# Two orderings moved in a two-layer attention and gated-MLP kernel: a first V pass of five contraction steps, and block 1's score sums held behind a layer norm

## The chip, the cores and the metric

The kernel runs on one core of a Trainium2 chip. The metric is the device time of one execution in microseconds (us); lower is better. Before the change it was 1618.4 us, the median of 3 executions (1618.09 to 1618.7). The profile's span (first to last instruction) is 1.7 to 2.0 us shorter than the device time in nearly all executions, and 2.6 to 2.7 us in three.

## The reference

Two layer pairs; each is attention over a dilated local window of 8 keys, then a gated MLP. S = 2048, D = 1024, F = 3584, 32 heads of 32.

```python
x = A_x
x = x + _A_ref(_layernorm(x), A_wqkv, A_wo)                    # q, k, v; 8 keys, 2 apart; softmax; @ wo
x = x + _B_ref(_layernorm(x), B_W_gate, B_W_up, B_W_down)      # (relu(x @ Wg) * (x @ Wu)) @ Wd
x = x + _A_ref(_layernorm(x), A_wqkv, A_wo)
x = x + _B_ref(_layernorm(x), B_W_gate, B_W_up, B_W_down)
return x
```

## The kernel before

The 2048 rows are worked on in four blocks of 512 rows (four tiles of 128 each). TensorE (PE) does all projections. VectorE (DVE) does the attention of one block while PE does the MLP of another. Q, K and V are the attention's input projections, Wo its output projection, LN2 the layer norm between Wo and the MLP; gate, up and down are the MLP's projections. PSUM is the memory that PE's products land in, and the other engines copy them out. The order on each engine is fixed by hand: `dv`, `mm` and `sp_dma` chain every operation behind the last one of its engine, and the program is emitted from a list of events with nominal times.

```python
def sp_dma(dst, src, transpose=False):
    start = nc.sync.dma_start_transpose if transpose else nc.sync.dma_start
    ...
        with tc.issue_after(tail_sp[0]):          # all these DMAs stand in ONE queue, in order
            tail_sp[0] = start(dst, src).ins
```

The start. Four tiles are normalised and turned (transposed) on PE, tile by tile; the V projection begins on tile 0 while the others are still being normalised.

```python
# ln_first: engine "v" is DVE, "a" is ACT, "g" is GpSimd
act_square(2)
act_mean(2)                       # ACT, two passes over tile 2
bn(1, 0)
apply(0, 0); apply(0, 1)          # normalise tile 0
turn(0)                           # 8 PE transposes
copy(0, "a", 0, 0, KC // 4)       # ACT copies the turned tile out of PSUM, in quarters
copy(0, "a", 0, KC // 4, KC // 2)
bn(1, 1); aggr(1)
copy(0, "v", 1)
act_power(2)
apply(1, 0); apply(1, 1)
...
def head():                       # V products of tile 0: contraction steps 0 to 3
    for kc in range(KC // 2):
        if kc == KC // 2 - 1:
            ln["second"](0)       # turn the first half of tile 1, copy it (DVE)
        for c in range(KC):
            prod(kc, c, 0, 1)
    ln["second"](1)               # turn the second half of tile 1
```

The V weights come in four pieces of two contraction steps each (512 KB): pieces 0 and 1, then x tile 3, then pieces 2 and 3.

Block 1's scores. `prod_sum_steps(1)` gives 16 steps; each is one multiplication of 128x2048 on DVE and mostly one addition, 2.2 to 2.3 us apiece. Steps 0 to 7 make the first half of the sums, 8 to 15 the second half. The second half is stored to DRAM and read back in another layout; head sums, softmax and the product with V follow.

```python
spread(sums1[:4], t_pv0 + 34.5, 4.5)
spread(sums1[4:6], t_wo0 + 0.5, 2.5)        # steps 4, 5: in front of the Wo additions
spread(sums1[6:10], t_fill + 1.4, 4.6)      # step 6: in front of tile 3's normalisation
spread(sums1[10:], t_gu0 + 2.6, 5.4)
...
# in gate/up of block 0; `at` is its start
ev.append((at + 37.5, store_s(1, 1)))       # second half of the sums -> DRAM
ev.append((at + 40.5, load_s(1)))           # read back, four DMAs
spread(gets2, at + 36.0, 2.5)               # block 2's q and k tiles
```

Weights come as slabs of 1 MB into a ring of five buffers. Gate and up each have seven slabs; a slab serves four of the 28 column groups of 128.

## Time and profile before

| before | value | read from |
|---|---|---|
| device time | 1618.4 us | 3 executions |
| PE busy | 1611.3 of 1616.4 us | busy table |
| 512-column matmul, start to start | 216 ns | trace |
| 256-column / 128-column matmul | 109 / 56 ns | trace |
| first Q matmul to last matmul | 1589.14 us | trace |

From the page of the kernel before: busy us (share of the span) and instructions of PE, and the chain of work that ended last, by engine.

```profile
PE 1611.3 (100%) x7633; PEld 786.6 (49%) x7633; DVE 1137.1 (70%) x960; ACT 475.8 (29%) x968; POOL 180.4 (11%) x168
...
PE 99%; DMA 0%; ACT 0%; DVE 0%; issue 0%; ACTq 0%; DVEq 0%
```

PE is the bound. The Trainium skill ("TensorE: Matmul & The Clock Gate", section "Wait — 56ns, not 53.3ns?") puts a warm matmul's start-to-start distance at N / 2.4 GHz plus about 2.5 ns and gives 215.7 and 55.6 ns as measured for 512 and 128 columns; for 256 columns an estimate from its formula is 109.2 ns. The trace's 216, 109 and 56 ns agree. Below, "against the pace" means: later than these distances allow. A change can gain only where PE falls behind that pace or has less to multiply.

The timeline of PE at the start (start in us, duration in us, engine, line, operation, out<-in, shape, count; in brackets the idle time before it and what ended it):

```profile
6.97 0.72 PE L385 MATMUL tp<-ident,xn_first 128*128 128x128 bf16 x8
8.09 1.50 PE L132 MATMUL acc_v<-xnT_first,w_v 128*128 128x128 bf16 x24 [0.40 <-ACT xnT_first L328]
9.51 0.40 PE L385 MATMUL tp_pair<-ident,xn_first 128*128 128x128 bf16 x4
9.74 0.61 PE L132 MATMUL acc_v<-xnT_first,w_v 128*128 128x128 bf16 x8
10.42 0.38 PE L385 MATMUL tp_pair<-ident,xn_first 128*128 128x128 bf16 x4
...
23.88 1.46 PE L132 MATMUL acc_q<-xnT_first,w_qk_q 128*128 128x512 bf16 x6
```

`tp` and `tp_pair` are the turns of tiles 0 and 1. The first V product waits for ACT's copy. Small waits follow before each half of tile 1's turn (9.51 and 10.42). Against the pace these are 0.55, 0.08 and 0.23 us.

The timeline of DVE around LN2 of block 0, with the same columns: the first Wo additions, the normalisations of tiles 1 and 3, and the last addition of the second sum.

```profile
168.77 2.48 DVE L106 TENSOR_TENSOR x<-acc_wo,x 128x512 bf16<-128x512 f32 x4
...
173.61 0.55 DVE L106 TENSOR_SCALAR xn_b<-x,mv,rstd 128x1024 bf16<-128x1024 bf16 x1 [0.73 <-POOL rstd L301]
...
185.35 0.54 DVE L106 TENSOR_SCALAR xn_b<-x,mv,rstd 128x1024 bf16<-128x1024 bf16 x1
...
228.38 2.29 DVE L106 TENSOR_TENSOR s<-ac,t 128x2048 bf16<-128x2048 f32 x1
```

### The profile page before, as it was taken

The numbers are of one execution on the slowest core, as the hardware profiler recorded it, in microseconds if no ns is written. First come the engines' busy times: TensorE is split into PE (matmuls) and PEld (weight loads), VectorE is DVE, ScalarE is ACT, GpSimd is POOL, SyncE is SP. The second block draws the span as 40 slices with busy tenths as digits, with TensorE's granted clock in tenths as the row PEclk, the third lists the DMA queues.
The fourth block names the chain that finished last, engine by engine and source line by source line (L and its number), as shares of the span: only waits on it lengthen the run. The fifth ranks groups of instructions, "written<-read, shape, count | busy, mean of one in ns | idle before, by whom it ended". The sixth has DMA issues, their size and how long they took to land.

```text
span 1616.4 us, 18930 instructions
## 1 busy us (share of the span) xinstructions
PE 1611.3 (100%) x7633; PEld 786.6 (49%) x7633; DVE 1137.1 (70%) x960; ACT 475.8 (29%) x968; POOL 180.4 (11%) x168
## 2 busy tenths in 40 slices
PE   9999999999999999999999999999999999999999
PEld 6646544444444445444454444544445444444444
DVE  5999989996989698929489293893939939311211
ACT  5853312132116313603136031361313311131110
POOL 2400100010003002300053000530005100000000
PEclk9999999999999999999999999999999999999999
DMA  9868868697669766794847947479574794755452
GB/s 306 180 190 238 224 159 262 183 216 204 208 192 217 200 184 212 192 246 146 227 160 201 240 153 230 152 205 252 165 226 155 203 245 157 209 161 177 157 167 68
DMA packets 407448, 317.92 MB, mean 197 GB/s; under 512 B 166464, under 2 KB 387008, under 8 KB 406848
## 3 DMA queue, kind: packets, MB, share of 16 engines
q1 hardware_dynamic: 406784, 316.13, 69.9%
q8 instruction: 59, 0.97, 0.3%
q10 hardware_dynamic: 576, 0.59, 0.1%
q14 instruction: 29, 0.24, 0.0%
HBM read 266.29 MB, written 34.66 MB: 186 GB/s over the span
## 4 chain that ended last, share of the span: by engine, by line
PE 99%; DMA 0%; ACT 0%; DVE 0%; issue 0%; ACTq 0%; DVEq 0%
PE acc_u L132 24%; PE acc_g L132 24%; PE dacc L132 18%; PE acc_v L132 7%; PE acc_wo L132 7%; PE acc_k L132 7%; PE acc_q L132 7%; PE dacc_pair L132 6%; DMA x<-in_A_x_dram 0%; ACT xn_first L328 0%; PE tp_pair L385 0%; PE L L132 0%; DVE x L837 0%; DVE xnT_first L106 0%; ACTq L175 0%
## 5 line engine op out<-in xcount | busy, mean ns | idle before, releaser
L132 PE MATMUL acc_g<-xnT_b,w_g 128*128 128x512 bf16 x1792 | 423.3, 379 | 0.0
L132 PE MATMUL acc_u<-xnT_b,w_u 128*128 128x512 bf16 x1792 | 423.3, 379 | 0.0
L790 ACT ACTIVATE r<-acc_g 128x512 bf16<-128x512 f32 x224 | 133.5, 596 | 726.7 <-PE acc_g L132 701.6
L106 DVE TENSOR_TENSOR hT<-acc_u,r 128x512 bf16<-128x512 f32 x224 | 150.5, 685 | 240.7 <-PE acc_u L132 238.2
L132 PE MATMUL dacc<-w_d,hT 128*128 128x512 bf16 (+1 forms) x1400 | 301.9, 375 | 0.0
L132 PEld LDWEIGHTS <-hT 128*128 128x128 bf16 x1820 | 178.1, 98 | 208.9
L132 PEld LDWEIGHTS <-w_u 128*128 128x128 bf16 x1792 | 175.3, 98 | 211.5
L132 PEld LDWEIGHTS <-w_g 128*128 128x128 bf16 x1792 | 175.4, 98 | 211.4
L106 DVE TENSOR_TENSOR pv<-a,vhm 128x4096 bf16<-128x4096 bf16 x64 | 143.4, 2281 | 0.0
L837 DVE TENSOR_TENSOR x<-dacc,x 128x512 bf16<-128x512 f32 (+1 forms) x38 | 24.5, 672 | 154.2 <-PE dacc L132 154.2
L608 DVE TENSOR_TENSOR t<-q,k 128x2048 f32<-128x2048 bf16 x56 | 128.0, 2292 | 6.7 <-ACT k L543 4.6
L106 DVE TENSOR_TENSOR t<-q,k 128x2048 f32<-128x2048 bf16 x56 | 127.4, 2285 | 3.7 <-ACT k L543 2.6
L106 DVE TENSOR_TENSOR pv<-pv 128x1024 bf16<-128x1024 bf16 (+1 forms) x128 | 113.6, 947 | 0.0
L549 POOL COPY kh<-k 128x14 bf16<-128x14 bf16 x40 | 56.0, 1406 | 504.3 <-ACT k L543 504.3
L132 PE MATMUL acc_wo<-w_o,oT 128*128 128x512 bf16 x512 | 111.8, 379 | 0.0
L621 DVE TENSOR_TENSOR ac<-ac,t 128x2048 f32<-128x2048 f32 x48 | 109.6, 2284 | 0.3
L106 DVE TENSOR_TENSOR ac<-ac,t 128x2048 f32<-128x2048 f32 x48 | 109.5, 2282 | 0.0
L264 POOL TENSOR_TENSOR st_b<-st_b,neg_half 128x1 f32<-128x1 f32 x29 | 43.9, 1523 | 525.8 <-ACT st_b L263 525.7
L132 PE MATMUL dacc_pair<-w_d,hT 128*128 128x512 bf16 x420 | 95.9, 379 | 0.0
L132 PEld LDWEIGHTS <-oT 128*128 128x128 bf16 x512 | 50.0, 98 | 60.4
L259 ACT ACTIVATE xn_b<-x 128x1024 bf16<-128x1024 bf16 x29 | 30.3, 1045 | 129.1 <-DVE x L106 67.0
L446 ACT CAST vT<-acc_v 128x512 bf16<-128x512 f32 x56 | 32.8, 588 | 57.6 <-PE acc_v L132 56.6
(134 smaller groups left out, 1230.0 us busy)
## 6 DMA issues: line engine op xcount, KB each, us to landing
w_g<-in_B_W_gate_dram SPq DMA_DIRECT2D x56, 1024.0 KB, 7.4
w_u<-in_B_W_up_dram SPq DMA_DIRECT2D x56, 1024.0 KB, 5.5
w_d<-in_B_W_down_dram SPq DMA_DIRECT2D x48, 1024.0 KB, 5.7
w_o<-in_A_wo_dram SPq DMA_DIRECT2D x16, 1024.0 KB, 7.0
vhm<-v_d SPq DMA_DIRECT2D x32, 284.0 KB, 6.8
v_d<-vT SPq DMA_DIRECT2D x8, 1024.0 KB, 9.8
oT<-o_d SPq DMA_DIRECT2D x32, 256.0 KB, 4.5
w_d<-in_B_W_down_dram SPq DMA_DIRECT2D x16, 512.0 KB, 3.9
```

The costliest lines, as they stand in the source:

```text
L106: tail_dve[0] = f(*args, **kwargs).ins
L132: tail_pe[0] = nc.tensor.matmul(*args, **kwargs).ins
L259: nc.scalar.activation(xn, xt[:], ACT.Square, accum_out=sq)
L264: nc.gpsimd.tensor_tensor(rstd, vpe, neg_half[:, 0:1], op=ALU.pow)
L446: tail_act[0] = nc.scalar.copy(st["vT"][:, c, :], acc[:]).ins
L549: nc.gpsimd.tensor_copy(khalo[n][:, c, :], k[:, BLK:BLK + HALO])
L608: nc.vector.tensor_tensor(t[:], i0, i1, op=ALU.mult)
L621: nc.vector.tensor_tensor(o, ac[:], t[:], op=ALU.add)
L790: tail_act[0] = nc.scalar.activation(rs[j][:], acc[:], ACT.Relu).ins
L837: run = dv if n < NB - 2 else (lambda f, *args, **kwargs: f(*args, **kwargs))
```

## The change

Its intent, at the start: let PE do a fifth contraction step of tile 0 where it waits for tile 1, so that eight later 256-column products shrink to 128 columns; take ACT's mean of tile 2 out of the way of the first copies. At LN2: let DVE do the Wo additions and normalisations of block 0 as soon as Wo's results come, and do block 1's sum steps 5 and 6 after that.

```diff
         act_square(2)
-        act_mean(2)
 ...
         copy(0, "a", 0, KC // 4, KC // 2)
+        act_mean(2)
         bn(1, 1)
         aggr(1)
         copy(0, "v", 1)
-        act_power(2)
 ...
             copy(1, "v", 1)
+            act_power(2)
             apply(2)
@@ head
-            for kc in range(KC // 2):
-                if kc == KC // 2 - 1:
+            for kc in range(KC // 2 + 1):
+                if kc == KC // 2:
                     ln["second"](0)
@@ second_half
-                        prod(kc, c, t0, t0 + 2)
+                        prod(kc, c, t0 + int((kc, t0) == (KC // 2, 0)), t0 + 2)
@@ block 1's sums
-    spread(sums1[4:6], t_wo0 + 0.5, 2.5)
-    spread(sums1[6:10], t_fill + 1.4, 4.6)
+    ev.append((t_wo0 + 0.5, sums1[4]))
+    spread(sums1[5:10], t_fill + 3.3, 3.4)
```

## The prediction

> **What bounds the kernel.** TensorE. The page's busy table gives PE 100% (1611.3 of 1616.4 us), DVE 70%; the chain that ended last is 99% PE. In the trace 512-column matmuls start every 216 ns, 256-column ones every 109, 128-column ones every 56. The Trainium skill ("TensorE: Matmul & The Clock Gate", section "Wait — 56ns, not 53.3ns?") gives N/2.4 GHz plus 2.5 ns, 215.7 and 55.6 ns; the trace agrees. From the first transpose on, places where PE ran over 40 ns behind that pace sum to about 1.1 us: 0.55 (first V product waits for ACT's first copy of tile 0, which stands behind the mean of tile 2), 0.08 among the transposes, 0.08 (tile 1's turn waits for its normalisation, 9.50 us), 0.23 (second half of the turn waits for DVE's copy of the first half, ending 10.36), 0.19 at the attention head sum. Wo, fill and gate/up of block 0 run at exactly 216 ns. The change can gain under 1 us.
>
> **First part.** ACT's mean of tile 2 (1.06 + 0.19 us, 6.63 to 7.77) moves behind the two copies. The fourth transpose starts at 7.15; with the 0.26 us that a copy takes to follow, the first copy runs about 7.41 to 7.75 and the first V product starts about 7.8 instead of 8.09. PE then has 32 products (1.79 us) instead of 24 before tile 1's turn, which starts about 9.6 (before 9.50): the wait is filled. The fifth contraction step (8 x 56 ns) needs the third piece of the V weights, landed at 10.14 in this trace, 0.3 us after PE would want it; so that step runs about 10.2 to 10.65 and the second half of the turn starts about 10.65 (before 10.42). Repaid later: eight 256-column matmuls become 128-column, 8 x 53 = 0.42 us. Net gain about 0.2 us (0.4 if the weights land early, 0 if late). Tile 2's normalisation moves from 11.2 to 12.7, needed at 14.2: harmless.
>
> **Second part.** Two DVE operations (4.5 us) go from before the Wo additions to after LN2, and another pair from before tile 3's normalisation to after it. DVE adds tile 0 at 164.4 instead of 168.8; the last transpose is issued about 178.5 instead of 185.9 (used at 190.3). PE did not wait there, so nothing is gained in this trace; margins grow (a PSUM buffer for Wo's last tile came free 0.1 us before its use). In exchange DVE waits for Wo tiles, so the held sums end about 1.1 us later (193.7, before 192.6), and the first gate product ends about 203.2; its PSUM buffer is needed at 204.1. Margin 0.9 us: no stall, but the closest risk.
>
> **Predicted time:** 1618.1 us (1618.4 - 0.2, perhaps 0.1 for margins), 80% range 1617.3 to 1619.0. Faster by over 2%: 0.005; within 2%: 0.99; slower by over 2%: 0.005.
>
> **What would show it.** Timeline: first V product at 7.8 us; a wait on the third V weight piece near 9.8 to 10.2; first Q product of block 0 about 0.2 us before 23.88. DVE: Wo additions from 164, last LN2 transpose issued before 180; block 1's first sums ending 1 us later; gate/up still at 216 ns.
>
> **What would make it wrong.** The third weight piece landing much later; DVE over 0.9 us further behind at the gate products, stalling PE 1 to 2 us; or unprofiled executions having stalls at Wo that the change removes (gain up to 1 us).

## More of the kernel before

The timeline of the DMA queue (SPq) during gate/up of block 0. For a DMA the duration is that of its issue.

```profile
218.57 0.53 SPq L121 DMA_DIRECT2D q<-q_d  x1
230.70 0.34 SPq L121 DMA_DIRECT2D s_d<-s  x1
...
233.90 4.38 SPq L121 DMA_DIRECT2D s<-s_d  x4
238.32 1.46 SPq L121 DMA_DIRECT2D q<-q_d  x1
239.88 0.39 SPq L121 DMA_DIRECT2D w_u<-in_B_W_up_dram  x1
```

The queue stands still from 219 to 230.7 us. It waits for DVE's second sum, which began at 228.38. The store, a k tile, the four read-backs and a q tile are issued next, and only then the up slab, at 239.88. This slab is the fifth of `w_u`. PE starts on it at 247.27, without a gap, in the timeline of PE:

```profile
245.54 1.89 PE L132 MATMUL acc_g<-xnT_b,w_g 128*128 128x512 bf16 x8
247.27 1.89 PE L132 MATMUL acc_u<-xnT_b,w_u 128*128 128x512 bf16 x8
```

The slab's last DMA engine reported at 246.88 us and PE loaded its first weights from it at 247.05 (landings and single matmuls are worked out from the trace's records here and below). The margin is 0.17 us in this execution.

## The result, and the profile after

The changed kernel took 1619.16 us, median of 6 executions (1618.38 to 1620.38); the kernel before took 1618.28 (1617.72 to 1618.7, 6 executions). The ratio is 1.0006, with a 95% interval of 0.9993 to 1.0019. A ratio is the mean time of one kernel's runs over that of the other's of the same rounds, so it is not quite the ratio of the medians quoted here. By the interval alone it is no difference; by the medians it is 0.9 us longer, and a repetition (below) gave 1.1 us. The profiled execution was the fastest of the six (1618.38 us), so it can show only a part of this. The median lies 0.16 us above the predicted range.

From the page after (busy row of PE, and the chain that ended last by engine):

```profile
PE 1608.1 (99%) x7592; PEld 786.4 (49%) x7641; DVE 1137.4 (70%) x960; ACT 475.8 (29%) x968; POOL 178.5 (11%) x168
...
PE 97%; DVE 1%; DMA 1%; SPq 0%; issue 0%; DVEq 0%
```

DVE and DMA have entered the chain with 1% each, and SPq is named, where the chain was 99% PE before. PE's busy time is not to be compared: this trace lacks matmul records (7592, against 7641 weight loads).

The timeline of PE at the start, after:

```profile
6.50 0.72 PE L385 MATMUL tp<-ident,xn_first 128*128 128x128 bf16 x8 [0.30 <-DVE xn_first L106]
7.36 1.95 PE L132 MATMUL acc_v<-xnT_first,w_v 128*128 128x128 bf16 x32
9.14 0.39 PE L385 MATMUL tp_pair<-ident,xn_first 128*128 128x128 bf16 x4
10.12 0.62 PE L132 MATMUL acc_v<-xnT_first,w_v 128*128 128x128 bf16 x8 [0.59 <-DMA w_v<-in_A_wqkv_dram]
10.57 0.39 PE L385 MATMUL tp_pair<-ident,xn_first 128*128 128x128 bf16 x4
...
23.61 1.67 PE L132 MATMUL acc_q<-xnT_first,w_qk_q 128*128 128x512 bf16 x7
```

The first 32 V products now run before tile 1's turn. The fifth step is the eight products at 10.12, and it waited for a piece of the V weights (0.59 us idle in the line; 0.75 us against the pace). The first Q product came at 23.61 instead of 23.88. This whole execution also started earlier: the first transpose was at 6.50 instead of 6.97. Counted from that transpose the first Q product came after 17.11 us, where it had been 16.91, so the 0.27 us on the clock are not a gain of the first part.

The timeline of DVE around LN2, after:

```profile
163.97 1.88 DVE L106 TENSOR_TENSOR x<-acc_wo,x 128x512 bf16<-128x512 f32 x3
166.05 0.69 DVE L106 TENSOR_TENSOR x<-acc_wo,x 128x512 bf16<-128x512 f32 x1 [0.20 <-PE acc_wo L132]
...
169.76 0.55 DVE L106 TENSOR_SCALAR xn_b<-x,mv,rstd 128x1024 bf16<-128x1024 bf16 x1 [1.39 <-POOL rstd L301]
...
177.81 0.55 DVE L106 TENSOR_SCALAR xn_b<-x,mv,rstd 128x1024 bf16<-128x1024 bf16 x1 [0.66 <-POOL rstd L301]
...
229.92 2.29 DVE L106 TENSOR_TENSOR s<-ac,t 128x2048 bf16<-128x2048 f32 x1
```

The Wo additions start at 163.97 instead of 168.77 and tile 3 is normalised at 177.81 instead of 185.35, as intended. But DVE now idles for a Wo tile (0.20 us) and longer for GpSimd: 1.39 us before tile 1's normalisation (0.73 before), 0.67 before tile 2's (0.66 before) and 0.66 before tile 3's (none before). These idle times grew by 1.53 us in all, and the second sum's last addition starts at 229.92 instead of 228.38. Against PE, which was 0.27 us earlier here, DVE is 1.8 us later.

The timeline of the DMA queue, after:

```profile
218.31 0.53 SPq L121 DMA_DIRECT2D q<-q_d  x1
232.24 0.34 SPq L121 DMA_DIRECT2D s_d<-s  x1
...
235.46 3.72 SPq L121 DMA_DIRECT2D s<-s_d  x4
239.23 1.26 SPq L121 DMA_DIRECT2D q<-q_d  x1
240.59 0.39 SPq L121 DMA_DIRECT2D w_u<-in_B_W_up_dram  x1
```

Everything behind the store has moved with it. The up slab is issued at 240.59, 0.98 us later against PE. That is less than DVE's 1.8 us, because in this execution the queue took 8.35 us from the store to the slab, where it took 9.18 in the kernel before (the read-backs alone 3.72 instead of 4.38). It landed at 247.50 us. The timeline of PE there, after:

```profile
245.28 1.89 PE L132 MATMUL acc_g<-xnT_b,w_g 128*128 128x512 bf16 x8
247.55 1.90 PE L132 MATMUL acc_u<-xnT_b,w_u 128*128 128x512 bf16 x8 [0.38 <-DMA w_u<-in_B_W_up_dram]
```

A gap has opened that was not there; against the pace it is 0.54 us. The waits of PE, after (us in total, times, longest):

```profile
PE acc_v L132 <- DMA w_v<-in_A_wqkv_dram: 0.6, 1, 0.6
PE acc_u L132 <- DMA w_u<-in_B_W_up_dram: 0.4, 1, 0.4
```

The balance of the profiled execution closes. From the start of the first Q matmul to the start of the last matmul it took 1589.70 us, where the kernel before took 1589.14. The difference, 0.56 us, is the gap at 247 within rounding. The first Q product was 0.27 us earlier on the clock; 0.56 - 0.27 gives 0.29 us, and the last matmul came at 1613.31 instead of 1613.02.

### The profile page after: what moved, and what is told of

The parts are those of the page before. It is cut to its first block, busy times and chain, and to the rows that moved or that the text cites. A ratio compares the mean times of both kernels' runs of the same rounds, so it can differ in the third digit from the quotient of the medians. Undisturbed runs are those within 1.5% of the kernel's fastest.

```text
span 1616.7 us, 18896 instructions
## 1 busy us (share of the span) xinstructions
PE 1608.1 (99%) x7592; PEld 786.4 (49%) x7641; DVE 1137.4 (70%) x960; ACT 475.8 (29%) x968; POOL 178.5 (11%) x168
## 4 chain that ended last, share of the span: by engine, by line
PE 97%; DVE 1%; DMA 1%; SPq 0%; issue 0%; DVEq 0%
PE acc_u L132 23%; PE acc_g L132 23%; PE dacc L132 18%; PE acc_q L132 7%; PE acc_k L132 7%; PE acc_wo L132 7%; PE acc_v L132 7%; PE dacc_pair L132 6%; DVE t L106 1%; DVE ac L106 1%; DMA w_u<-in_B_W_up_dram 0%; DMA w_v<-in_A_wqkv_dram 0%; SPq L121 0%; DMA s_d<-s 0%; DVE s L106 0%
```

## The experiments

Twelve kernels ran, each five times, with nine executions of the kernel before on the same chip; kernels with the same number in the third column share these nine. All were correct. Theory A: the held sums make DVE late, and the store that waits for DVE stands at the head of an in-order DMA queue in front of the up slab. Theory B: the first pass loses, by its wait for the third piece of the V weights, and the rest is noise.

| kernel | median us (range) | before, same chip | ratio (95%) |
|---|---|---|---|
| whole change, again | 1619.20 (1618.35 to 1619.78) | 1618.07 | 1.0005 (0.9992 to 1.0017) |
| first part alone | 1618.11 (1617.64 to 1619.26) | 1618.07 | 1.0000 (0.9988 to 1.0013) |
| second part alone | 1618.93 (1618.53 to 1620.02) | 1618.07 | 1.0004 (0.9991 to 1.0018) |
| change, two slabs in front of the store | 1622.33 (1621.44 to 1622.65) | 1618.07 | 1.0024 (1.0011 to 1.0037) |
| before, up slab later in the queue | 1618.61 (1618.46 to 1620.11) | 1617.92 | 1.0006 (0.9992 to 1.0020) |
| first part, one sum step held | 1618.52 (1618.42 to 1619.13) | 1617.92 | 1.0004 (0.9992 to 1.0017) |
| change, up slab in front of the store | 1618.14 (1617.78 to 1618.89) | 1617.92 | 1.0001 (0.9989 to 1.0014) |
| one step held, up slab and third piece early | 1617.74 (1617.47 to 1617.82) | 1617.92 | 0.9998 (0.9985 to 1.0011) |
| before, up slab in front of the store | 1618.28 (1617.67 to 1618.63) | 1618.27 | 1.0000 (0.9988 to 1.0013) |
| first part, third piece early | 1618.14 (1617.69 to 1618.74) | 1618.27 | 1.0000 (0.9986 to 1.0013) |
| change, up slab and third piece early | 1617.80 (1617.31 to 1618.13) | 1618.27 | 0.9997 (0.9984 to 1.0010) |
| first part, up slab and third piece early | 1618.26 (1617.90 to 1618.74) | 1618.27 | 1.0000 (0.9988 to 1.0013) |

Only the fourth row's interval excludes 1. The device times alone would settle little, so the next table gives what the profiled execution of each kernel shows. The columns are worked out from the traces: the landing of the piece of the V weights with contraction steps 4 and 5 (its last DMA engine), the first Q matmul, their difference, and the time from the first Q matmul to the last matmul.

| kernel | piece landed | first Q | Q - landing | last matmul - Q |
|---|---|---|---|---|
| before | 10.14 | 23.88 | 13.74 | 1589.14 |
| second part alone | 11.21 | 24.04 | 12.83 | 1589.93 |
| before, up slab later | 10.42 | 23.44 | 13.02 | 1590.08 |
| before, up slab in front | 10.82 | 24.07 | 13.25 | 1589.14 |
| whole change | 10.07 | 23.61 | 13.54 | 1589.70 |
| whole change, again | 10.04 | 23.64 | 13.60 | 1589.93 |
| first part alone | 10.35 | 23.89 | 13.54 | 1589.14 |
| first part, one step held | 10.99 | 24.54 | 13.54 | 1589.14 |
| change, up slab in front | 10.02 | 23.56 | 13.54 | 1589.14 |
| change, two slabs in front | 10.76 | 24.30 | 13.54 | 1592.19 |
| one step held, both repairs | 9.80 | 23.34 | 13.54 | 1589.14 |
| first part, third piece early | 10.32 | 23.86 | 13.54 | 1589.14 |
| change, both repairs | 10.29 | 23.83 | 13.54 | 1589.14 |
| first part, both repairs | 10.50 | 24.05 | 13.55 | 1589.14 |

Two constants stand out. Without a gap, everything after the first Q takes 1589.14 us, also with DVE 1.8 us late. With the first part of the change, the first Q comes 13.54 us after the third piece lands, in nine of ten profiled executions (13.55 counted with them), and 13.60 in the tenth. One thing is not constant: the margin of the fifth up slab. In the two other kernels that have the store and the slab at their old places and DVE on time ("first part alone" and "first part, third piece early") the slab landed 1.06 and 0.70 us before its use, where it was 0.17 in the kernel before; the queue took 8.49 and 8.54 us from the store to the slab there.

### The whole change again

No edit.

> The changed kernel again, for the same chip as the next three. Theory A (the held sums make DVE late, the store of block 1's second sum waits for DVE at the head of SP's in-order queue, and the load of the fifth up slab stands behind it and lands late): 0.5 to 1.5 us over the kernel before, a PE gap of 0.3 to 2 us in front of the first up product of that slab at about 247 us, and a wider spread than before because the landing varies. Theory B (the first pass loses: the third piece of the V weights is waited for, the rest is noise): the same total, but no gap at 247 is needed.

Measured: 1619.20 us against 1618.07, 1.1 us over, a gap of 0.77 us at 247 and the slab landed at 247.76. The spans of its five executions are 1616.6 to 1618.1 us. The size of the loss repeats. This profile, too, is of one of the faster executions (1618.64 us). The gap's size varies from one execution to the next; it was 0.54 and 0.77 us in the two that were profiled.

### First part alone

```diff
-    ev.append((t_wo0 + 0.5, sums1[4]))
-    spread(sums1[5:10], t_fill + 3.3, 3.4)
+    spread(sums1[4:6], t_wo0 + 0.5, 2.5)
+    spread(sums1[6:10], t_fill + 1.4, 4.6)
```

> First part of the change alone; the sums stand as in the kernel before. Theory A: 0.2 to 0.3 us below the kernel before (about 1618.0), PE waits 0.6 to 0.8 us for the third V piece near 9.5 us and none over 0.2 us at 247. Theory B: as slow as the whole change, 0.5 to 1 us over before.

Measured: 1618.11 against 1618.07. The wait for the third piece is there (0.63 us against the pace) and there is no gap at 247; the slab landed at 246.01. By medians and by the profile (1589.14 us after the first Q) the first part does not lose, so theory B falls. It does not gain 0.2 to 0.3 us either: that much of my expectation was wrong.

### Second part alone

The kernel before with the last hunk of the change.

> Second part alone. Theory A: slower than before by 0.8 to 1.5 us (it lacks the start's 0.27 us), the up product at 247 waits for its weights 0.5 to 2 us, the store of the second sum is issued near 232.2 instead of 230.7. Theory B: equal to before within 0.2 us.

Measured: 1618.93, 0.86 us over before. The store is issued at 232.70, the slab landed at 248.16, and the gap is 0.66 us. The loss is in this part. In this execution PE also lost 0.10 us in Wo, which explains the rest of the 0.79 us over 1589.14, to 0.03 us.

### First attempt at a repair: two slabs in front of the store

```diff
-            ev.append((at + 37.5, store_s(1, 1)))
-            ev.append((at + 40.5, load_s(1)))
+            ev.append((at + 42.0, store_s(1, 1)))
+            ev.append((at + 42.1, load_s(1)))
```

> The whole change, with the store and the loads of block 1's second sum moved behind the fifth up slab and the sixth gate slab in SP's queue; DVE and PE keep their order. Theory A: the up slab is issued near 230 instead of 240.6, the gap at 247 is gone, 0.2 to 0.4 us below before (1617.9 to 1618.1) and a spread as narrow as before's. Theory B: as slow as the whole change.

Measured: 1622.33, 4.3 us over before. The gap at 247 is gone, but others of 0.6, 1.2 and 1.2 us opened at 258, 272 and 317. The timeline of this kernel's DMA queue:

```profile
230.62 0.38 SPq L121 DMA_DIRECT2D w_u<-in_B_W_up_dram  x1
232.34 0.38 SPq L121 DMA_DIRECT2D w_g<-in_B_W_gate_dram  x1
232.95 0.40 SPq L121 DMA_DIRECT2D s_d<-s  x1
241.99 3.43 SPq L121 DMA_DIRECT2D s<-s_d  x4
```

The store was issued at 232.95, and the read-backs that wait for it could be issued only at 241.99. In the changed kernel the same step took from 232.24 to 235.46. Two slabs of 1 MB were in front of 512 KB, and the second of them was issued only 0.61 us before the store and landed at 239.91. The head sums on DVE started at 250.78 instead of 244.52, DVE was 6 us later from there on, and PE waited for DVE instead (waits of PE, same columns as above):

```profile
PE acc_u L132 <- DVE hT L106: 1.5, 2, 1.1
...
PE acc_wo L132 <- DVE x L106: 1.0, 1, 1.0
```

The Trainium skill states both halves of this, in general terms. "DMA: Bandwidth & Descriptors", section "Anatomy of one DMA — SWDGE (gpsimd) path", says that "DMA engines do not wait on semaphores — any semaphore wait happens on the issuing sequencer before dispatch"; the section is on another engine's path, but the sentence is of DMA engines in general. In the changed kernel SyncE's queue stood from 218.8 to 232.2 us in front of one store. Section "Queues, rings and completion order" says that on each DMA engine descriptors are consumed in ring order, though a later one may finish before an earlier one. In this experiment the store landed about 9 us after issue behind the two slabs, against about 3 us in the changed kernel. The traces agree with both and prove neither. My expectation had looked at the first half only.

### Before, with the up slab later in the queue

DVE is left alone; two of block 2's tiles are put in front of the slab.

```diff
-            spread(gets2, at + 36.0, 2.5)
+            spread(gets2[:3], at + 36.0, 2.5)
+            spread(gets2[3:5], at + 41.2, 0.2)
+            spread(gets2[5:], at + 48.5, 2.5)
```

> The kernel before with one edit: two of block 2's reloads (a k and a q tile) stand in front of the load of the fifth up slab in SP's queue instead of behind the sixth gate slab. DVE's order is untouched. If it is the queue place of that load that costs (theory A): DVE's second sum still ends at its old time (store near 230.7), the slab is issued 1.5 to 3 us later than 239.9, PE has a gap of 1 to 3 us at 247 us, the kernel is 1 to 3 us over before. If DVE's lateness costs by some other way: equal to before within 0.3 us.

Measured: 1618.61 against 1617.92, 0.7 us over, and a gap of 0.93 us at 247. From its DMA queue (the store and the up slab) and its waits of PE:

```profile
230.28 0.34 SPq L121 DMA_DIRECT2D s_d<-s  x1
...
240.69 0.38 SPq L121 DMA_DIRECT2D w_u<-in_B_W_up_dram  x1
```

```profile
PE acc_u L132 <- DMA w_u<-in_B_W_up_dram: 0.8, 1, 0.8
```

The store is at 230.28, 206.84 us after the first Q, where it was 206.81 in the kernel before: DVE is not late. The slab is issued 217.25 us after the first Q (before 216.00), and the gap appears. So the slab's place in the queue is enough to make the gap. Loss and gap lie just below the 1 to 3 us that I had expected: the slab was issued 1.25 us later against PE, where I had guessed 1.5 to 3.

### First part, and one of the two sum steps held

```diff
-    spread(sums1[6:10], t_fill + 1.4, 4.6)      # first part of the change, old sums
+    spread(sums1[6:10], t_fill + 3.3, 3.4)
```

> First part of the change, and of the second part only one of its two moves: the sum pair that stood in front of tile 3's normalisation goes behind it, the pair in front of the Wo additions stays. DVE then fills the Wo time as before. Theory A: no lateness, the second sum's store within 0.3 us of 230.7, no gap over 0.25 us at 247, time equal to the first part alone (0 to 0.2 us under before). If holding any sum costs: 0.5 us or more over the first part alone.

Measured: 1618.52 against 1617.92. There was no gap at 247 in the profiled execution (1589.14 us after Q). But DVE did become late, by 0.87 us against PE: the store stood 207.68 us after the first Q. From its timeline of DVE, tile 3's normalisation and the last addition of the first sum:

```profile
182.34 0.55 DVE L106 TENSOR_SCALAR xn_b<-x,mv,rstd 128x1024 bf16<-128x1024 bf16 x1 [0.66 <-POOL rstd L301]
...
191.85 2.29 DVE L106 TENSOR_TENSOR s<-ac,t 128x2048 bf16<-128x2048 f32 x1
```

Step 6 had filled the wait for GpSimd before tile 3's normalisation. With it gone, DVE idles 0.66 us there. So my expectation that DVE would not be late was wrong. The slab's landing left little margin: 222.89 us after Q, where PE needs it at 223.17 (247.05 - 23.88 in the kernel before). The profiled execution (1618.85 us) took 0.66 us longer than that of before to its last matmul, all of it in front of the first Q product (24.54 against 23.88; the third piece landed at 10.99). Why the median is 0.6 us over before could not be separated, as the other executions have no trace. That is about the 0.5 us over the first part alone that I had named as the sign that holding any sum costs, so this experiment does not exclude such a cost.

### The whole change, with only the up slab in front of the store

```diff
+            when = t_gu0 + 38.2 if key == ("u", 0, 4) else ...     # slab_events
-            ev.append((at + 37.5, store_s(1, 1)))
+            ev.append((at + 38.3, store_s(1, 1)))
```

> The whole change with only the fifth up slab's load put in front of the store of the second sum (the earlier repair put 2 MB of weights there and the store landed 9 us after issue). Theory A with the DMA engines shared in order: slab issued near 230.6, no gap at 247; the store lands 1 to 2 us later than in the changed kernel, the head sums start near 246 instead of 244.6, and the time is 0.3 us under to 0.7 us over before. If the store still lands 5 us or more late, gaps of 1 us appear after 257 as in the earlier repair.

Measured: 1618.14 against 1617.92, and 1.1 us less than the whole change in its earlier run on the same chip (0.9 us less, each against its own runs of before). The timeline of its DMA queue:

```profile
229.88 0.37 SPq L121 DMA_DIRECT2D w_u<-in_B_W_up_dram  x1
232.21 0.34 SPq L121 DMA_DIRECT2D s_d<-s  x1
...
236.45 3.61 SPq L121 DMA_DIRECT2D s<-s_d  x4
```

The slab uses the time in which the queue would have stood still. The store's read-backs start 4.24 us after the store instead of 3.22. There is no gap after the first Q: 1589.14 us. DVE is as late as in the whole change (store at 232.21), and it costs nothing any more. This is the opposite test to the one with the slab later: with DVE late and the slab early, the loss is gone.

### One step held, with the up slab and the third piece early

```diff
-    load_x(0, [TPB - 1])
-    load_slab(("v0", 1), qkv_half(2, 1))
+    load_slab(("v0", 1), qkv_half(2, 1), lambda: load_x(0, [TPB - 1]))   # x tile 3 between pieces 2 and 3
```

together with the edit of the last experiment, on the kernel with one sum step held.

> Attempt at a better kernel: first part, one-move hold, fifth up slab in front of the second sum's store, and the third piece of the V weights loaded before x tile 3. If the first part's gain was eaten by the wait for that piece: the wait of 0.15 to 0.9 us near 9.5 us is gone, the first Q product comes near 23.2 instead of 23.6 to 23.9, and with no gap at 247 the kernel is 0.5 to 0.8 us under before. If the piece was not the cause: Q within 0.15 us of 23.7 and no gain.

Measured: 1617.74 against 1617.92. The timeline of PE at its start:

```profile
7.51 2.01 PE L132 MATMUL acc_v<-xnT_first,w_v 128*128 128x128 bf16 x32 [0.24 <-ACT xnT_first L330]
9.36 0.39 PE L387 MATMUL tp_pair<-ident,xn_first 128*128 128x128 bf16 x4
9.84 0.62 PE L132 MATMUL acc_v<-xnT_first,w_v 128*128 128x128 bf16 x8
...
23.34 1.89 PE L132 MATMUL acc_q<-xnT_first,w_qk_q 128*128 128x512 bf16 x8
```

The fifth step starts at 9.84, with 0.25 us lost in front of it, and the first Q is at 23.34. Its span median is 1615.9 us against 1616.2 of before. It is the lowest median but not clear of noise, and far from the 0.5 to 0.8 us under before that I had expected.

### Four more, to see what each repair is worth

Before, with only the up slab in front of the store:

> The kernel before with only the fifth up slab in front of the second sum's store. In the profile of before that slab landed 0.17 us before its use, so some unprofiled executions may have waited for it. If so: 0.1 to 0.3 us under before and a narrower spread. If before never waited: equal within 0.1 us. The start is not touched, so the first Q product does not follow the third V piece's landing by a fixed time.

Measured: 1618.28 against 1618.27. The kernel before does not wait for this slab in a way that shows in five executions.

First part and the third piece early, nothing else:

> First part of the change and the third V piece loaded before x tile 3; sums and the up slab's queue place as in before. In all five kernels with the first part the first Q product came 13.54 to 13.60 us after that piece landed, so if the piece bounds the start: it lands near 9.4 to 9.8, Q comes 13.5 to 13.7 us after it, 0.2 to 0.5 us earlier than with the first part alone; PE then reaches the up product at 247 so early that it waits up to 0.5 us there, and the time is 0 to 0.4 us under before. If the piece does not bound: Q as with the first part alone, 23.6 to 23.9.

Measured: 1618.14 against 1618.27. The first Q follows the piece by 13.54 us again. But in this execution the piece landed at 10.32, no earlier than at its old place in other executions: the DMA stream as a whole was later (piece 1 was also waited for, 0.40 us). So the first Q product's fixed distance to the piece is shown, and the gain from the earlier place is not.

The whole change and both repairs:

> The whole change with both repairs (up slab in front of the store, third V piece before x tile 3). If the loss of the change came from those two waits alone: no gap at 247, no wait over 0.3 us at the start, 0.2 to 0.6 us under before. If holding both sum pairs costs by itself (DVE late by 1.8 us against PE): gaps at the gate products or at Wo of block 1, and slower than the kernel with the first part and the two repairs.

Measured: 1617.80 against 1618.27. No gap, 1589.14 us after Q. The longest wait at the start was 0.40 us, in front of the first V product; I had expected none over 0.3.

First part and both repairs, sums as before:

> First part and both repairs, sums as in before. If the held sums are worth nothing once the queue is repaired: equal to the whole change with both repairs within 0.2 us, 0.2 to 0.6 us under before. If holding helps: 0.2 us or more slower than that kernel.

Measured: 1618.26 against 1618.27. It is 0.46 us slower than the kernel above by medians, which is what I had named as the sign that holding helps. The profiles do not show it: both take 1589.14 us after the first Q, and their first Q products differ by 0.22 us, with the landing of the piece. So no gain of the held sums is seen in the profiles, and the 0.46 us stay unexplained, within the intervals. The two kernels that came out lowest (1617.74 and 1617.80) are 0.2 and 0.5 us under before; neither is shown to be faster.

## Why the prediction was wrong

**PE bounds, and under 1 us is to be had.** Right. The kernel before loses only at the start and at the head sum, and 1589.14 us after the first Q repeats in nine kernels.

**First part: the mechanism.** Right. The first V product came 0.86 us after the first transpose (7.36 - 6.50), predicted 0.83; the wait in front of it was 0.29 us against the pace, where the predicted 7.8 us implies about 0.26; the predicted wait for the third piece appeared.

**First part: the size.** Over-estimated, within the bounds I gave. I predicted 0.2 us net, "0.4 if the weights land early, 0 if late". Alone it measured 0.04 us over before. The term that was mis-sized is the wait for the piece: I had put it at 0.3 us, and 0.15 to 0.92 us were measured in six profiled executions that load the piece at its old place. I had taken one landing, 10.14, as if it were fixed. It varied from 10.02 to 11.21 us between executions, and PE's first transpose from 6.50 to 7.05 us in the six. With the first part, the first Q product hangs on that landing (13.54 us). From the first transpose to the first Q product the six took 16.60 to 17.79 us, the four kernels with the old start 16.91 to 17.63: no gain is visible.

**Second part: "no stall, but the closest risk".** This is the step that failed. I followed DVE's lateness to one place, the PSUM buffers behind the gate products, and found a margin of 0.9 us. That held: no gap appeared there. DVE's lateness reached PE by another way. The store of the second sum waits for DVE, it stands in the in-order DMA queue, and the fifth up slab stands behind it with a margin of 0.17 us in the profile that I had. The gap was 0.54, 0.77 and 0.66 us in three profiled executions. Removing it by the slab's place alone took the whole change from 1619.2 to 1618.1 us (0.9 us, each against its own runs of before); making it by the slab's place alone, with DVE on time, took the kernel before from 1617.9 to 1618.6.

**Second part: DVE's lateness.** Under-sized. I predicted 1.1 us; it was 1.54 us on the clock (229.92 against 228.38) and 1.8 against PE. The cause that I gave, waiting for Wo tiles, made 0.20 us of it. The rest is GpSimd: 0.66 us more before tile 1's normalisation, because GpSimd worked on tile 0's statistics first in the new order, and 0.66 us before tile 3's, which step 6 had filled.

**"Last LN2 transpose issued before 180".** Wrong: 184.25 (before 185.91). Tile 3 was normalised by 178.4, but the four transposes stand in the DMA queue. It waited until 176.4 for a k product of PE (3.1 us) before it issued the first of them, then worked through three transposes, a v tile and two stores of k tiles with pauses of 0.1 us or less, and reached the fourth at 184.25. It is the same oversight: I moved an operation forward by its data and not by its queue.

**The range.** Its upper end was 1619.0, and the median was 1619.16. I had allowed for a stall only as an unlikely event at the gate products.

What stays open: how large the gap is in executions without a profile. The whole change's median span exceeds that of before by 1.1 us on the same chip (1617.5 against 1616.4), more than the gaps in its two profiles, which are both of faster executions. That the difference is the same gap at other sizes is inferred from the repair, not seen.

## What to carry to other kernels

When an operation is made later, follow every queue that waits for it, not only the buffers that it frees: a store that waits for a late engine holds back all the loads behind it in an in-order DMA queue, and those can belong to another stage. Before trusting "there is no gap here", look for how late the data landed before its use; a margin of 0.17 us is a gap that has not opened yet, and one profile does not tell the margin: it was 0.17, 0.70 and 1.06 us in three. And when moving a load in front of a latency-critical store, move as little as needed: with 1 MB in front the store landed 1 us later after its issue, with 2 MB 6 us, and that cost the kernel 4. (The 2 MB were also issued closer to the store, so amount and spacing are not separated.)

## What the Trainium skill lacked or had wrong

- "DMA: Bandwidth & Descriptors" says where a DMA waits for a semaphore (on the issuing sequencer), but I found no warning there of the consequence: DMAs behind it in that queue are held although their own data and buffers are ready. Here the up slab's buffer was free by 230 us (issued at 229.88 when put in front), and in the whole change it was issued at 240.59.
- The same page has no figure for how much the landing of the same DMA varies between executions. Here the third piece of the V weights, at its old place in the queue, landed between 10.02 and 11.21 us in ten profiled executions (issued at 3.2 to 3.6).
- "TensorE: Matmul & The Clock Gate" agreed with the traces: 216 and 56 ns for 512 and 128 columns, and 109 ns for 256 by its formula. Nothing was found wrong.
